# Four middle blocks of a retention-plus-MLP kernel: part of the first layer as seven products, and the next batch's retention all in the second layer

## The chip, the cores and the metric

One core of one Trainium2 chip. The metric is the device time of one execution of the whole kernel, in microseconds; three runs of the kernel before gave 293.72 us as the median (293.19 to 295.14). Inputs are float32, the matmuls work in float16 and accumulate in float32.

## The reference

Eight batches of eight heads, 576 positions, head width 64. Retention is attention without softmax, with a decay per head; its output, laid out as 4608 tokens of 512 values, goes through two weight matrices with a GELU between them:

```python
scores = (q @ k.T) / 8 ; ret = scores * Dmat        # Dmat[i, j] = gamma_h ** (i - j) for i >= j, else 0
x = (ret @ v).transpose(0, 2, 1, 3).reshape(4608, 512)
h = x @ w_in                                        # 512 x 2048
out = gelu_tanh(h) @ w_out                          # 2048 x 512
```

## The kernel before

The 4608 tokens are nine blocks of 512 (`NTB` = 9, counted t = 0 to 8). Block t below 8 holds the first 512 positions of batch t; block 8 holds the remaining 64 positions ("tails") of all eight batches. While TensorE runs the two layers of block t, the retention of batch t+1 is woven in between, so that `xT`, the retention's output, is there when block t+1 begins.

**First layer.** `up` (line 474) makes one of 16 column slices f of 128: four matmuls over 512 tokens into a bank `hp`, and a GELU on ScalarE into `gT`. Slices f and f + 8 belong together. Blocks 7 and 8 (`WIN`, line 514) make three of their four column groups (a group is two low and two high slices) in Strassen-Winograd form instead: `up_prod` (line 554) makes seven products of four matmuls over 256 tokens each, numbered 1 to 7, from sums of weight parts (`in_sums`, line 518) and of input parts (`x_sums`, line 535). Products share banks: 1, 6, 7, 4 accumulate one after the other in `hB`, 5 and 3 in `hC`, 2 is in `hA`. Between two of them the bank's intermediate value is read out: after 1 and 6 by a ScalarE copy, after 7 by a VectorE copy; VectorE then adds the other banks and ScalarE applies the GELU. `W_ORDER` (line 848) writes the order out by hand: "06" is product 6 of group 0, an empty token is one plain `up`, "a" and "b" are the sums below, "Q" a second-layer product.

**Second layer.** Always in seven products (`prod`, line 648), each two halves of eight matmuls over 256 columns; four sums per pair of slices prepare the left sides (`act_sums`, lines 642 to 646: s1, s2, a difference in place in `gT`, and s4). In blocks 1 to 6 the order is 1, 6, 5, 7, 2, 4, 3 (line 1036). Products 6, 7 and 4 accumulate in the one bank `opB`; after 6 VectorE adds it into k2 (line 721), after 7 into k3 and the output (lines 726 and 728), after 4 into the other output half.

**Retention of the next batch.** Four chunks of 128 positions, two at a time. `score` (line 379) takes two PSUM banks a chunk; `masks` (line 389) multiplies each by the decay mask on VectorE and so frees it; `past` and `av` (lines 436 and 455) make `xs` from the carried state `tbd` and the masked scores; `put` (line 466) copies `xs` to `xT` on ScalarE; `state`, `scan` and `spread` (lines 402, 416, 430; the last two together are `later`, line 784) carry the state from chunk to chunk, `spread` on ScalarE. There are eight PSUM banks, handed out in the order in which they were dropped (`bank`, line 61).

**What sets the order.** Every engine runs its instructions in the order of emission, and that order is written by hand. A block's steps are numbered u = 0 to 15 in the first layer and 16 to 29 in the second (one half product each); `at(t, u, f)` hangs work behind step u of block t. For blocks 2 to 6 line 949 puts the first two chunks' scores at u = 11 (blocks 2 and 3) or 9, their reads and the other two chunks' scores at 15, those masks at 17 and 19 and their reads at 24. So half of the masks, and the state of the first three chunks, fall into the first layer.

**Loads.** All float32 inputs arrive through one queue (SP) into a ring of 16 tiles of 128 x 512 (`LD`, tag "ld", line 71); `pump` (line 141) issues the next load as soon as a cast has freed a tile. The 12 tiles of batch b are cast during the second layer of block b - 2 from u = 16 on (`ut`, line 970): keys and queries on GpSimd, values on ScalarE. A tiny GpSimd copy, the `gate` (line 979), first waits for the last s4 sum. DMA transposes (`turn_dma`, line 305) follow. Tails of two batches come as further loads (`load_tails`), are cast on GpSimd behind the batches 4, 5 and 7 and in block 6 (`cast_tails`), and add their own scores, masks and reads in blocks 3, 4, 6 and 7 (`TP`, line 132).

Of the kernel before, what the change touches and what calls it, by code (L numbers as in the profile page):

```python
# [20 lines left out]
def kernel(  # L21
# [23 lines left out]
    LD = 16  # L45
# [3 lines left out]
    NT4 = 4  # L49
    scale = 1.0 / math.sqrt(D)  # L50
# [18 lines left out]

    def lds():  # L70
        return sb.tile([128, 512], F32, tag="ld", name="ld", bufs=LD)

# [66 lines left out]
    q_ld = {"next": 0, "free": LD, "hold": False}  # L139

    def pump(freed=0):
        q_ld["free"] += freed
        while q_ld["next"] < len(seq) and not q_ld["hold"]:
# [5 lines left out]
            if s[0] != "t":  # L149
                if q_ld["free"] == 0:  # L150
                    return
                q_ld["free"] -= 1
# [103 lines left out]
    def cast(b, key, c, eng):  # L256
        a = att[b]
        raw = a["raw"].pop((key, c))
# [255 lines left out]
    WIN = {t: 3 for t in (NTB - 2, NTB - 1)}  # L514
    GW = max(WIN.values())
    wi = {}

    def in_sums(j, ns):
        if not wi:
            for g in range(0, GW, 2):  # L520
                for n in "234":
                    wi[n, g // 2] = sb.tile([128, 2, 512], F16, tag="ld", name="wi" + n, bufs=LD)
# [12 lines left out]
    def x_sums(t):  # L535
        if not xw:
            for n in ("12", "34"):
                x = sb.tile([128, 2, 4, 2, TL], F16, tag="ld", name="x" + n, bufs=LD)
                xw[int(n[0])], xw[int(n[1])] = x[:, 0], x[:, 1]
            for n in range(3):  # L540
                for s in "svu" if n < 2 else "vu":
                    wk[s, n] = sb.tile([128, 512], F32, tag="ld", name="w" + s, bufs=LD)
# [3 lines left out]
        for s, x, y, f in (  # L546
# [3 lines left out]
            nc.vector.tensor_tensor(out=s, in0=x, in1=y, op=f)  # L550

    wk, wb, due = {}, {}, []

    def up_prod(t, j, m):
# [23 lines left out]
        s, v, u3 = wk["s", j % 2], wk["v", j % 3], wk["u", j % 3]  # L578
# [55 lines left out]
    def act_sums(t, f0, f1, us=slice(0, 2), parts=(0, 1)):  # L634
# [6 lines left out]
        if 0 in parts:  # L641
            nc.vector.tensor_tensor(out=s["1"], in0=a21, in1=a22, op=ALU.add)  # L642
            nc.vector.tensor_tensor(out=s["2"], in0=s["1"], in1=a11, op=ALU.subtract)
            nc.vector.tensor_tensor(out=a21, in0=a11, in1=a21, op=ALU.subtract)  # L644
        if 1 in parts:
            nc.vector.tensor_tensor(out=s["4"], in0=a12, in1=s["2"], op=ALU.subtract)  # L646
# [25 lines left out]
    def after(t, m, u):  # L672
# [46 lines left out]
        elif m == 6:  # L719
            keep["u2"] = sb.tile([128, 2, HD], F32, tag="k2", name="k2", bufs=1)  # L720
            add(keep["u2"], keep["s1"], pr("B"))
            for f in range(0, NH if t in WIN else 0, 2):
                act_sums(t, f, f + 2, parts=(1,))
        elif m == 7:
# [35 lines left out]
    def cast_w(kind, *i):  # L760
# [11 lines left out]
        pump(1)  # L772
# [4 lines left out]
    def cc(b, key, c, eng):  # L777
        cast(b, key, c, eng)
        pump(1)
# [70 lines left out]
    ).replace("p", "").split(" ")  # L850
    for n in range(GW):
        at(NTB - 3, 17 + 2 * n, lambda n=n: in_sums(n, (3, 2)))
        at(NTB - 3, 18 + 2 * n, lambda n=n: in_sums(n, (4, 1)))
    at(NTB - 3, 27, lambda: x_sums(NTB - 2))
# [60 lines left out]
    for t, b in TP.items():  # L915
        at(t, 3, lambda b=b: tail_values(b))
# [30 lines left out]
    for t in range(1, B):  # L947
        b, tl = t + 1, TP.get(t)
        s0, o0, s1, o1 = U2 if t == 1 else (11 if t in (2, 3) else 9, 15, 15, 24)
        at(t, s0, lambda t=t, tl=tl: scores(t, 0, tl))  # L950
# [5 lines left out]
        else:  # L956
            at(t, s1, lambda b=b: (score(b, 2), score(b, 3)))
            at(t, 17, lambda b=b: masks(b, 2))
            at(t, 19, lambda b=b: masks(b, 3))
# [7 lines left out]
    for b in range(NPE, B):  # L967
# [3 lines left out]
        if b == NPE + 1:  # L971
            ut = [16, 16, 17, 19, 19, 20, 22, 22, 23, 24, 24, 25]
        if b == NPE:
# [17 lines left out]
    for t in range(NTB):  # L991
# [9 lines left out]
        else:  # L1001
# [7 lines left out]
            todo = deque(f + h for f in range(2 * WIN.get(t, 0), NH) for h in (0, NH))  # L1009
            for w in (W_ORDER if t in WIN else ()):  # L1010
# [7 lines left out]
                def token(w):  # L1018
# [5 lines left out]
                    elif w[0] in "ab":  # L1024
                        act_sums(t, 2 * int(w[1]), 2 * int(w[1]) + 2, parts=("ab".index(w[0]),))
                    else:
                        up_prod(t, int(w[0]), int(w[1]))
                steps.append((mixed, 0 if w[:1] in ("a", "b", "Q") else 1 if w else 2))
# [56 lines left out]
```

## Time and profile before

| what | value |
|---|---|
| median of three runs | 293.72 us (293.19 to 295.14) |
| the profiled execution | 293.76 us |
| its span | 292.0 us |
| granted TensorE clock, mean | 0.996 |
| block 3, first plain group to the next block's | 114.70 to 145.31 us |
| block 4 | 145.31 to 175.76 us |
| block 5 | 175.76 to 205.53 us |
| block 6 | 205.53 to 236.16 us |
| block 7, three groups as products | 236.16 to 262.13 us |
| GpSimd busy | 100.0 us of the span (34%) |

The span runs from the first to the last instruction of the profiled execution; the device time is a little longer. The block limits are the starts of their first matmuls in the chain of waits. A timeline line reads: start, duration (or of several in a row, their total), engine, source line, operation, output <- inputs, shapes, count, and in square brackets how long the engine stood idle before it and who released it. PE is TensorE, DVE VectorE, ACT ScalarE, POOL GpSimd, SP the queue of the loads. Instructions of one engine overlap at their edges, so several in a row take less than the sum of their durations.

### The profile page before, as it was taken

To read this page: it belongs to the slowest core of one execution; us is meant where nothing else is said; L and a number is where in the kernel's file an instruction comes from. 1 tells how busy PE (TensorE), PEld (TensorE's weight loads), DVE (VectorE), ACT (ScalarE), POOL (GpSimd) and SP (SyncE) were. 2 spreads that over 40 slices of the span, in tenths; PEclk is the share of its full clock that TensorE was granted. 3 is DMA by queue.
4 is the path that set the end of the run, shared out by engine and by line. 5 is a ranking of instruction groups with operands and counts; after the bars stand their busy time and mean duration, and the time that the engine had idled before them with its cause. 6 is when DMAs were issued, how large, how long until landed. Compare 5 with 4: busy or idle time off the path is not lost.

```text
span 292.0 us, 7383 instructions
## 1 busy us (share of the span) xinstructions
PE 280.1 (96%) x3024; PEld 207.6 (71%) x3024; DVE 204.1 (70%) x409; ACT 169.8 (58%) x321; POOL 100.0 (34%) x128
## 2 busy tenths in 40 slices
PE   6889998999999999999999999999999999999993
PEld 2558877888874687468845884488548887887783
DVE  7796998666864874477548834784489968974863
ACT  5487754987249545964396647664666258507810
POOL 4589779910661175008500730068030000000000
PEclk9999999999999999999999999999999999999998
DMA  6999999989999999999999979997952030003013
GB/s 195 308 382 370 364 293 228 252 213 163 225 192 230 235 206 183 244 235 210 200 267 209 218 147 270 216 190 99 271 95 38 2 144 3 0 21 125 3 36 108
DMA packets 139585, 53.95 MB, mean 185 GB/s; under 512 B 118048, under 2 KB 131360, under 8 KB 139552
## 3 DMA queue, kind: packets, MB, share of 16 engines
q1 hardware_dynamic: 138960, 52.97, 80.4%
q8 instruction: 23, 0.38, 0.6%
q10 hardware_dynamic: 592, 0.52, 0.5%
q14 instruction: 10, 0.08, 0.1%
HBM read 36.70 MB, written 9.44 MB: 158 GB/s over the span
## 4 chain that ended last, share of the span: by engine, by line
PE 66%; SPq 8%; DMA 8%; ACT 5%; POOL 5%; DVE 5%; issue 1%; POOLq 0%; DVEq 0%; ACTq 0%
PE hp L480 18%; PE opB L665 11%; PE opA L665 8%; PE opC L665 7%; SPq L101 5%; DMA ld<-in_moe_w_in_dram 4%; PE hp L501 4%; PE hB L574 3%; SPq L96 3%; ACT gT L486 3%; PE xs L459 2%; POOL w_out_sb L771 2%; PE st L383 2%; DMA ld<-in_v_dram 2%; DMA ld<-in_q_dram 2%; PE hC L574 2%
## 5 line engine op out<-in xcount | busy, mean ns | idle before, releaser
L480 PE MATMUL hp<-xT,w_in_sb 128*128 128x512 f16 x352 | 79.1, 379 | 0.6 <-ACT xT L469 0.3
L486 ACT ACTIVATE gT<-hp 128x512 f16<-128x512 f32 x88 | 50.1, 600 | 22.6 <-PE hp L480 22.0
L480 PEld LDWEIGHTS <-w_in_sb 128*128 128x128 f16 x352 | 34.0, 98 | 39.0 <-issue 1.1
L665 PEld LDWEIGHTS <-gT 128*128 128x128 f16 x576 | 54.9, 98 | 8.9 <-issue 0.9
L665 PEld LDWEIGHTS <-s 128*128 128x128 f16 x432 | 42.2, 98 | 4.9
L642 DVE TENSOR_TENSOR s<-gT 128x512 f16<-128x512 f16 x36 | 15.6, 434 | 31.2 <-ACT gT L486 24.5
L665 PE MATMUL opA<-w_out_sb,gT 128*128 128x256 f16 x288 | 36.0, 273 | 0.6 <-ACT w_out_sb L771 0.4
L392 DVE TENSOR_TENSOR ret<-st,cm 128x512 f16<-128x512 f32 x48 | 30.2, 681 | 3.6 <-PE st L383 3.6
L469 ACT CAST xT<-xs 128x512 f16<-128x512 f32 x36 | 19.2, 590 | 20.4 <-PE xs L459 17.0
L501 PE MATMUL hp<-xT,w_in_sb 128*128 128x256 f16 x256 | 29.9, 273 | 0.9 <-POOL w_in_sb L771 0.5
L275 POOL TENSOR_TENSOR ck<-ld,sc 128x512 f16<-128x512 f32 x24 | 25.0, 1043 | 9.7 <-DMA ld<-in_k_dram 9.7
L501 PEld LDWEIGHTS <-w_in_sb 128*128 128x128 f16 x256 | 24.3, 98 | 5.2 <-POOL w_in_sb L771 2.3
L434 ACT CAST tbd<-ws 64x256 f16<-64x256 f32 x48 | 19.4, 403 | 14.8 <-DVE ws L425 14.2
L275 POOL TENSOR_TENSOR cq<-ld,sc 128x512 f16<-128x512 f32 x24 | 26.1, 1088 | 2.6 <-DMA ld<-in_q_dram 2.1
L665 PE MATMUL opB<-wt,gT 128*128 128x256 f16 x224 | 26.8, 273 | 0.0
L979 POOL COPY gate<-s 128x1 f16<-128x1 f16 x5 | 0.9, 190 | 74.6 <-DVE s L646 74.6
L262 ACT CAST cv<-ld 128x512 f16<-128x512 f32 x24 | 14.2, 618 | 17.2 <-DMA ld<-in_v_dram 17.1
L508 ACT ACTIVATE gT<-hp 128x512 f16<-128x512 f32 x32 | 18.3, 605 | 3.5 <-PE hp L501 3.3
L679 DVE TENSOR_TENSOR k<-k,opB 128x512 f32<-128x512 f32 x17 | 11.7, 686 | 11.7 <-PE opB L665 10.7
L644 DVE TENSOR_TENSOR gT<-gT 128x512 f16<-128x512 f16 x36 | 18.0, 499 | 0.0
L665 PE MATMUL opB<-wt,s 128*128 128x256 f16 x144 | 17.4, 273 | 0.0
L665 PE MATMUL opC<-wt,s 128*128 128x256 f16 x144 | 17.2, 272 | 0.0
(122 smaller groups left out, 406.4 us busy)
## 6 DMA issues: line engine op xcount, KB each, us to landing
ld<-in_q_dram SPq DMA_DIRECT2D x32, 256.0 KB, 5.2
ld<-in_k_dram SPq DMA_DIRECT2D x32, 256.0 KB, 5.1
ld<-in_v_dram SPq DMA_DIRECT2D x32, 256.0 KB, 5.3
out_dram<-ost SPq DMA_DIRECT2D x16, 512.0 KB, 3.9
ld<-in_moe_w_in_dram SPq DMA_DIRECT2D x16, 256.0 KB, 5.7
ld<-in_moe_w_out_dram SPq DMA_DIRECT2D x16, 256.0 KB, 5.6
lt<-in_k_dram SPq DMA_DIRECT2D x8, 128.0 KB, 4.7
lt<-in_q_dram SPq DMA_DIRECT2D x8, 128.0 KB, 4.4
```

Of the source, the lines that this page charges most:

```text
L101: nc.sync.dma_start(out=t.rearrange("p (h d) -> p h d", d=D), in_=src[b, :, 128 * c : 128 * c + 128, :].rearrange("h s d -> s h d"),)
L275: eng.tensor_tensor(out=dst.rearrange("p (h d) -> p h d", d=D), in0=raw.rearrange("p (h d) -> p h d", d=D), in1=sc[:, s0].unsqueeze(2).to_ ...
L392: nc.vector.tensor_tensor(out=r.rearrange("p (n i) -> p n i", i=128), in0=t.rearrange("p (n i) -> p n i", i=128), in1=(cm if b < PAIR else ...
L434: cp(out=(tbd[b % 2][r, c, :, r] if c < NC - 1 else tbt[b % NT4][r, :, r]), in_=w[r])
L469: nc.scalar.copy(out=xT[:, g0 : g0 + 2], in_=xs.rearrange("p (n g t) -> p g n t", n=HP, g=2))
L480: nc.tensor.matmul(hp.rearrange("p (g t) -> p g t", t=TL), w_in_sb[:, ct, 128 * fc : 128 * fc + 128], xT[:, o : o + TB // TL, ct, :], star ...
L486: nc.scalar.activation(out=gT[t][:, fc].rearrange("p i n -> p (i n)"), in_=hp, func=AF.Gelu_apprx_tanh)
L501: nc.tensor.matmul(hps[n][:, 256 * x : 256 * x + 256].rearrange("p (g t) -> p g t", t=TL), w_in_sb[:, ct, 128 * (fs[n] + x) : 128 * (fs[n] ...
L508: nc.scalar.activation(out=gT[t][:, f : f + 2, 2 * u : 2 * u + 2, :].rearrange("p f i n -> p f (i n)"), in_=hp.rearrange("p (f n) -> p f n ...
L642: nc.vector.tensor_tensor(out=s["1"], in0=a21, in1=a22, op=ALU.add)
L644: nc.vector.tensor_tensor(out=a21, in0=a11, in1=a21, op=ALU.subtract)
L665: nc.tensor.matmul(op[tag][:, HD * u : HD * u + HD], lhs(f), rhs[:, f], start=(new and f == 0), stop=(f == NH - 1), skip_group_check=True,)
```

## The change

Five things, all for blocks 3 to 6 (`MID`), with consequences in block 2 and in the rings.

1. **First layer.** Two of the four column groups become seven products each; the other eight slices stay plain. The order is `M_ORDER`: four plain slices, then products, then plain slices in between. A token such as "c21" is part of `act_sums` on VectorE: "c" is s1 and s2, "d" the difference in `gT`, the first digit is half of the first slice, the second half of the number of slices. After the last first-layer matmul come c01, c11, c31, d02, d31; s4 of all slices moves behind product 6 of the second layer.
2. **x sums** of these blocks run on GpSimd, hung at u = 0. Those of blocks 7 and 8 stay on VectorE.
3. **Retention** of the next batch moves into the second layer: scores of the first two chunks (and tails) at 15, their masks at 17, reads and the other scores at 22, those masks at 23 and 24, their reads at 26. The casts of the batch after next go from u = 16 to 20 and on.
4. **Weight sums** of the first two groups (`in_sums`) move from block 6 to block 2 (u = 17 to 20); the third stays in block 6. They stay on VectorE.
5. **Rings.** The ring of 16 becomes two of 8 ("ld", "lm"), taken in turn for the weights and batches 0 to 3; from batch 4 on only "ld" is used, and "lm" holds the weight sums, the x sums and work tiles of the products. The work tiles of group 0 share buffers with k1, k2 and k3.

Block 7's hand-written order gets one plain slice moved to its front. The core of the diff:

```diff
-    LD = 16
+    LD = 8
+    FIRST = 3
...
-                if q_ld["free"] == 0:
+                tag = "ld" if s[0] == "b" and s[1] >= FIRST + 1 else ("ld", "lm")[q_ld["n"] % 2]
+                if q_ld["free"][tag] == 0:
                     return
...
+    MID = {t: 2 for t in range(FIRST, NTB - 2)}
...
-            nc.vector.tensor_tensor(out=s, in0=x, in1=y, op=f)
+            (nc.gpsimd if t in MID else nc.vector).tensor_tensor(out=s, in0=x, in1=y, op=f)
...
+        def work(s):
+            n = j % (2 if s == "s" else 3)
+            if n == 0 and m == {"s": 1, "v": 6, "u": 7}[s]:
+                wk[s, 0] = sb.tile([128, 512], F32, tag=KT[s], name=KT[s], bufs=1)
+            return wk[s, n] if (s, n) in wk else None
...
             for f in range(0, NH if t in WIN else 0, 2):
                 act_sums(t, f, f + 2, parts=(1,))
+            for f in range(0, NH if t in MID else 0, 4):
+                act_sums(t, f, f + 4, parts=(1,))
...
+    M_ORDER = "    01 c21 02 05 11 06 12 d21  15 07 16  04 17 03  14 13  c01 c11 c31 d02 d31".split(" ")
     for n in range(GW):
-        at(NTB - 3, 17 + 2 * n, lambda n=n: in_sums(n, (3, 2)))
-        at(NTB - 3, 18 + 2 * n, lambda n=n: in_sums(n, (4, 1)))
-    at(NTB - 3, 27, lambda: x_sums(NTB - 2))
+        t, u = (FIRST - 1, 17 + 2 * n) if n < 2 else (NTB - 3, 15 + 2 * n)
+        at(t, u, lambda n=n: in_sums(n, (3, 2)))
+        at(t, u + 1, lambda n=n: in_sums(n, (4, 1)))
+    for t in MID:
+        at(t, 0, lambda t=t: x_sums(t))
+    at(NTB - 3, 29, lambda: x_sums(NTB - 2))
...
-        at(t, 3, lambda b=b: tail_values(b))
+        at(t, 16 if t in MID else 3, lambda b=b: tail_values(b))
...
-        s0, o0, s1, o1 = U2 if t == 1 else (11 if t in (2, 3) else 9, 15, 15, 24)
-        at(t, s0, lambda t=t, tl=tl: scores(t, 0, tl))
+        s0, o0, s1, o1 = U2 if t == 1 else (15, 22, 22, 26) if t in MID else (11 if t == 2 else 9, 15, 15, 24)
+        if t in MID:
+            late = [(b, 0), (b, 1)] + ([(PAIR + tl, 0)] if tl is not None else [])
+            at(t, s0, lambda late=late: [score(*w) for w in late])
+            at(t, 17, lambda late=late: [masks(*w) for w in late])
+        else:
+            at(t, s0, lambda t=t, tl=tl: scores(t, 0, tl))
...
-            at(t, 17, lambda b=b: masks(b, 2))
-            at(t, 19, lambda b=b: masks(b, 3))
+            at(t, s1 + (1 if t in MID else 2), lambda b=b: masks(b, 2))
+            at(t, s1 + (2 if t in MID else 4), lambda b=b: masks(b, 3))
...
+        if t0 in MID:
+            ut = [u + 4 for u in ut]
```

## The prediction

> **What bounds the kernel now.** I read the page's shares first, then the busy time of each engine block by block, then the chain of waits through block 4, then VectorE's and ScalarE's timelines of the same block, and last the places where GpSimd runs beside VectorE. A profiled execution took 293.76 us: a span of 292.0 us and 1.76 us around it. The median of the three runs is 293.72 us, so the sum below is made on 293.76 and serves for both.
>
> ```profile
> span 292.0 us, 7383 instructions
> ...
> PE 280.1 (96%) x3024; PEld 207.6 (71%) x3024; DVE 204.1 (70%) x409; ACT 169.8 (58%) x321; POOL 100.0 (34%) x128
> ```
>
> TensorE is busy for 96%. By blocks (block 4 and block 6 here; columns are the sum, then PE, PEld, DVE, ACT, POOL) it has no hole in the blocks that the change edits:
>
> ```profile
> 145.30:175.80 30.50, 30.50 (x310) 21.02 (x308) 18.92 (x38) 18.84 (x36) 8.96 (x10) 1.00 1.00 211
> ...
> 205.50:236.20 30.70, 30.43 (x295) 20.76 (x293) 25.04 (x54) 16.67 (x32) 2.48 (x2) 1.00 0.42 92
> ```
>
> So a shorter first layer pays only if the other engines still answer in time. The chain of waits through block 4 (start, us, what) gives the prices: a plain matmul over 512 columns goes at 8.63 / 40 = 0.216 us, a product matmul over 256 at 0.109 us.
>
> ```profile
> 145.31 8.63 PE hp L480 x40
> 153.95 0.78 PE st L383 x24
> 154.72 5.29 PE hp L480 x24
> ...
> 163.91 1.75 PE opB L665 x16
> 165.66 1.75 PE opC L665 x16
> 167.41 1.75 PE opB L665 x16
> ...
> 236.16 0.44 PE hB L574 x4
> ```
>
> The second opB entry is product 7. It accumulates onto the bank of product 6, so it may start only when VectorE has read product 6 out (the add into k2, line 721). VectorE's timeline shows that read today:
>
> ```profile
> 154.40 2.47 DVE L392 TENSOR_TENSOR ret<-st,cm 128x512 f16<-128x512 f32 x4
> 156.79 1.28 DVE L392 TENSOR_TENSOR ret<-st,tm 128x512 f16<-128x512 f32 x2
> ...
> 163.75 1.28 DVE L392 TENSOR_TENSOR ret<-st,cm 128x512 f16<-128x512 f32 x2
> 165.77 0.69 DVE L679 TENSOR_TENSOR k<-k,opB 128x512 f32<-128x512 f32 x1 [0.74 <-PE opB L665]
> ```
>
> The add waited for TensorE (0.74 us) and ended at 166.46, 0.95 us ahead of product 7. That 0.95 us is all the slack there is.
>
> **The work saved.** A plain column group is 16 x 0.216 = 3.45 us, as seven products 28 x 0.109 = 3.06 us. Eight groups change: 8 x 0.39 = **-3.1 us**. Four VectorE operations of 0.69 us and two ScalarE copies of 0.58 us come with each group. The four x sums of a block stand on GpSimd (nearest rows: its cast 0.61, its product 1.04 us; I take 1.04, it has two inputs). They end some 4 us into a block, where product 5 wants the first at 4.3 us: priced at nothing, covered by the four plain groups in front; each us past 4.3 would cost one.
>
> **Blocks 3 to 6, step by step.** ScalarE and VectorE at the start of block 4, and nine GELUs back to back (4.74 / 9 = 0.53 us apiece, 0.49 in the pair):
>
> ```profile
> 89.98 4.74 ACT L486 ACTIVATE gT<-hp 128x512 f16<-128x512 f32 x9
> ...
> 149.20 1.09 ACT L486 ACTIVATE gT<-hp 128x512 f16<-128x512 f32 x2
> ```
>
> ```profile
> 150.32 0.42 DVE L642 TENSOR_TENSOR s<-gT 128x512 f16<-128x512 f16 x1 [3.03 <-ACT gT L486]
> 150.78 0.42 DVE L643 TENSOR_TENSOR s<-s,gT 128x512 f16<-128x512 f16 x1
> 151.12 0.42 DVE L644 TENSOR_TENSOR gT<-gT 128x512 f16<-128x512 f16 x1
> ```
>
> I count r from the block's first matmul. Undisturbed, TensorE needs 8 x 0.865 + 14 x 0.437 = 13.0 us for the first layer, then 0.78 us of scores (0.55 without tails) and 1.75 us each for products 1, 6, 5; product 7 would start at r = 19.1.
>
> Step 1, ScalarE in the first layer. Block 4 ends its fourth GELU at 150.29 (r = 5.0), behind two pairs of state copies. The copy of product 1 then ends near 5.5, and product 6 of the same group may write its bank only after that; it is ready at 5.2. Next, VectorE has the sums of f 4 and 5 in front of the first product add, so the second copy ends near 8.1 while product 7 of the first layer is ready at 7.7. 0.35 + 0.4 = 0.75 us a block, **+3.0 us** in four (0 as in block 7, which runs the same product order without a gap of over 0.1 us but without state copies; 6 if VectorE is further behind).
>
> Step 2, the read-out of product 6. The last first-layer product ends at r = 12.9 and its add at 13.7. Its GELU stands on ScalarE behind five others whose first can start at 12.3; at 0.5 us apiece it ends at 15.5. Only then can VectorE go on, in its order: sums of f 2 and 3 (0.80: 150.32 to 151.12), of f 6 and 7 (0.80), the differences over eight tiles (0.85, from the 0.884 of a 128x1024 sum on line 630) and over four (0.35), the four masks (2.4, from 154.40 to 156.79), the two tail masks (1.2), and then the add into k2 (0.69). Behind that add stand the last s sums, and GpSimd's casts of the next batch wait for those. 15.5 + 7.1 = 22.6. TensorE is ready at 19.1 + 0.75 = 19.85. It waits 2.7 us in blocks 3, 4 and 6; in block 5, which has no tail masks, 1.7. Rounded down a little for the 128x1024 estimate: 2.6 x 3 + 1.7 = **+9.5 us** (6 to 11).
>
> Step 3, banks. Behind half of product 7 stand the reads (three xs banks, one us bank) and four score banks, with three banks still held by opA, opB and opC: the last score waits for ScalarE's copies of xs to xT (0.48 us apart, 1.56 for three): 0.4 us in three blocks, **+1.2 us** (0 to 2).
>
> Step 4, the state of the next chunk. It is now computed after the second score, not before the second layer. From the end of product 7: the k3 add and the output add behind it 0.09 + 0.72 + 0.61, two masks 1.2, vs 0.45, ws 0.42 (1.23 beside a cast on GpSimd), two copies to tbd 0.82, and 0.08 of handing over: 4.4 to 5.2 us. TensorE has product 2, half of product 4 and one read in that time: 1.75 + 0.87 + 0.22 = 2.85. It waits 1.5 to 2.3 us for the tbd of line 434; behind those copies ScalarE still has two value casts and the xT that the next block begins with, which then come just ahead of it (r = 34.6 to 35.2 in a block of some 35.4). GpSimd is still casting in blocks 3 to 5 (its gate waits for the s sums, r = 24.3, and eight casts follow), so 1.9 x 3 + 1.5 = **+7.2 us** (5 to 9).
>
> **Block 2.** Two thirds of the weight sums move here from block 6, where nothing waited for them, so nothing is won there. In block 2 GpSimd casts at the same time. What that does, tail casts beside sums in block 6:
>
> ```profile
> 213.60 0.42 DVE L643 TENSOR_TENSOR s<-s,gT 128x512 f16<-128x512 f16 x1
> 213.94 1.26 DVE L644 TENSOR_TENSOR gT<-gT 128x512 f16<-128x512 f16 x1
> 215.13 1.26 DVE L646 TENSOR_TENSOR s<-gT,s 128x512 f16<-128x512 f16 x1
> ```
>
> ```profile
> 213.64 2.48 POOL L275 TENSOR_TENSOR e<-lt,sc 128x512 f16<-128x512 f32 x2 [10.49 <-DMA lt<-in_k_dram]
> ```
>
> An f16 sum goes from 0.42 to 1.26 us beside a cast, one for one. Four such sums now stand ahead of the add into k2. Two beside casts and two free are 2 x 1.2 + 2 x 0.4 = 3.2 us, less the 0.74 us idle and 0.95 us slack: 1.5 us, and 0.8 us for the second four ahead of the k3 add: **+2.3 us** (0.5 if all run free, 4.5 if none does).
>
> **What I price at nothing.** Blocks 7 and 8 keep their products; one plain group moves to the front of block 7. No DMA is added, but loads 9 to 12 of batches 5 to 7 stand on SP behind GpSimd's first casts, and tail loads, one output and the transposes behind those. With the gate at r = 24.3 the last casts end near 33, the tail casts near 37, the transposes land some 8 us into the next block and the scores read them at 13.8: covered by some 6 us, past which each us costs one. The x sums would start near 37, with the block 35 us long: 2 us into the next block, first one done at 3, wanted at 4.3.
>
> Sum: -3.1 + 3.0 + 9.5 + 1.2 + 7.2 + 2.3 = +20.1 us, **313.9 us**.
>
> **Rivals.**
> Faster: VectorE reaches the add into k2 by r = 19.8. For it: its busy share is only 70% now, and block 7, with three product groups, shows no lasting gap. Against it: block 7 has no masks of the next batch there and reads products 4 and 2 ahead of 6. All waits have to stay below 3.1 / 4 = 0.78 us a block to decide; with none the time is 293.76 - 3.1 = 290.7. Chance 0.06; about no change 0.03.
>
> Mild: VectorE falls behind by less, because ScalarE's last GELU comes near 14 instead of 15.5 (its rows back to back are 0.49 us). Steps 2 and 4 halve: 20.1 - 8.35 = +11.75, or 305.5; with steps 1 and 3 at 0 and block 2 at 0.5 (6.0 less) 299.5. With shorter blocks the x sums come late instead (37 against a block of 32: the first at 6, wanted at 4.3, so 1.7 us in blocks 4 and 6), which keeps the low end from going lower. Chance 0.17.
>
> Worse: the TensorE clock. After the last matmul (line of the windows: stretch, sum, matmuls, granted clock) it averages 0.74; from the first filler on, with no hole over 0.8 us, it is 1.00.
>
> ```profile
> 288.00:292.00 4.00, 0.00 (x0) 0.74 0.59 179
> ```
>
> A wait of 2.7 us may let it fall. If the 128x256 matmuls then cost 0.218 us for as long as the wait itself, each of the three waits adds 1.35 us: +4; for the remaining 10 us of each block, +15: 318 to 329. The Trainium skill (TensorE: Matmul & The Clock Gate, section What's actually happening) says that the clock is halved after one idle window of about 3.4 us and needs as long a busy one to return. By that rule the waits here stay just under the window, and the trace, which has no such hole, cannot show it. Chance 0.10.
>
> The forecast itself, 305.5 to 322: chance 0.64. A measurement of this kernel can tell about 1% from no change. The range of **302 to 323** takes in the forecast, half of the mild case and the near end of the clock case, some 0.78 together. Slower by over 1%: 0.91; within 1%: 0.03; faster: 0.06.
>
> **What would show it.** Step 2: in blocks 3 to 6 opB (product 7) idle before it, put down to the DVE k add, some 2 us each; the six masks in one row directly ahead of that add. Step 4: the xs read of the last chunk (line 450 now) waits for ACT tbd, 1.5 to 2.3 us. Step 1: hB waits for the ACT copies, under 0.5 us each. Block 2: wi sums of 1.2 us and a later second opB. Blocks of some 35 us (33 for block 5) instead of 30.5. I am wrong if opB follows opC without a hole, if masks run before the last sums, or if TensorE waits mainly for GpSimd's x sums or for loads.

## The result, and the profile after

| what | before | after |
|---|---|---|
| median of four runs | 293.50 us | 320.43 us (317.60 to 321.30) |
| ratio after to before, 95% interval | | 1.0888 (1.0806 to 1.0971) |
| the profiled execution | 293.76 us | 319.68 us |
| block 2 | 30.27 us | 31.69 us |
| blocks 3, 4, 5, 6 | 30.45, 30.45, 29.77, 30.63 | 37.22, 38.35, 34.27, 35.61 |
| block 7 | 25.97 us | 26.75 us |

The kernel is slower by 26.9 us. The direction and the range were right, the predicted 313.9 us are 6.5 us short. Ratios leave out disturbed executions; among the runs below this touches one execution of one kernel. Block limits here and below are the starts of each block's first matmul in the timeline. Line numbers below are those of each kernel's own program; of the changed kernel, masks are line 404, the adds of the second layer 700, the activation sums 667, the state copies 446, the ScalarE copies of products 1 and 6 of the first layer 615 and 621.

The page of the changed kernel, its span and first row:

```profile
span 317.8 us, 7666 instructions
...
PE 283.8 (89%) x3120; PEld 217.2 (68%) x3120; DVE 224.3 (71%) x429; ACT 175.3 (55%) x337; POOL 119.2 (38%) x144
```

TensorE is busy for hardly longer than before (280.1 us), and the span is 25.8 us longer: nearly all of it is standing still. The list of TensorE's waits (who waited, for whom: total us, times, longest) says where:

```profile
PE opB L686 <- DVE k L700: 7.7, 5, 1.8
PE xs L462 <- ACT tbd L446: 7.6, 5, 1.9
PE hB L589 <- ACT k L621: 3.1, 5, 1.4
...
PE hB L589 <- ACT k L615: 2.0, 4, 1.0
PE st L395 <- ACT xT L481: 1.1, 4, 0.3
```

The first row is step 2 (four times) and block 2 (once), the second step 4, the third and fourth step 1, the last a part of step 3. None of the first, third and fourth was there before; the second stood at 0.8 us in one place. By blocks 3 to 5 (window, its length, then PE, PEld, DVE, ACT, POOL busy, granted clock, DMA share, GB/s):

```profile
115.55:152.77 37.22, 31.17 (x335) 23.20 (x333) 24.77 (x43) 19.23 (x38) 16.16 (x17) 1.00 0.86 171
152.77:191.12 38.35, 32.71 (x335) 24.28 (x333) 24.82 (x44) 20.08 (x41) 16.19 (x17) 0.96 0.71 146
191.12:225.39 34.27, 30.53 (x310) 22.40 (x308) 22.17 (x41) 19.10 (x39) 11.87 (x13) 1.00 0.87 176
```

TensorE now has 4 to 6 us of holes in each, where it had none; no other engine comes near being full. The holes come from the order on VectorE. Its timeline in block 3, around the end of the first layer:

```profile
132.55 0.42 DVE L667 TENSOR_TENSOR s<-gT 128x512 f16<-128x512 f16 x1 [0.61 <-ACT gT L606]
...
134.15 1.02 DVE L667 TENSOR_TENSOR gT<-gT 128x1024 f16<-128x1024 f16 x2
135.08 2.47 DVE L404 TENSOR_TENSOR ret<-st,cm 128x512 f16<-128x512 f32 x4
137.48 1.28 DVE L404 TENSOR_TENSOR ret<-st,tm 128x512 f16<-128x512 f32 x2
138.67 0.67 DVE L700 TENSOR_TENSOR k<-k,opB 128x512 f32<-128x512 f32 x1
139.27 1.28 DVE L667 TENSOR_TENSOR s<-gT,s 128x1024 f16<-128x1024 f16 x2
144.28 0.69 DVE L700 TENSOR_TENSOR k<-k,opB 128x512 f32<-128x512 f32 x1 [3.73 <-PE opB L686]
```

The late sums, six masks, the add into k2 and the last s sums: one row of work without a gap, as predicted, 8.0 us long (132.55 to 140.55), and straight behind it 3.73 us in which VectorE has nothing to do. TensorE in the same block, product 7 and the last chunk's read of the past:

```profile
139.40 1.03 PE L686 MATMUL opB<-wt,gT 128*128 128x256 f16 x8 [1.68 <-DVE k L700]
...
148.99 0.40 PE L462 MATMUL xs<-tt,tbd 128*128 128x128 f16 x4 [1.90 <-ACT tbd L446]
```

And the clock in block 4, in windows of 1 us (the last three columns: granted clock, DMA share, GB/s):

```profile
185.00:186.00 1.00, 0.24 (x4) 0.23 (x4) 1.00 (x2) 0.96 (x3) 0.75 (x1) 1.00 0.00 0
186.00:187.00 1.00, 1.00 (x23) 0.91 (x22) 0.05 (x1) 1.00 (x3) 0.00 (x0) 0.59 0.00 0
187.00:188.00 1.00, 1.00 (x21) 0.81 (x18) 0.00 (x0) 1.00 (x3) 0.00 (x0) 0.50 0.07 16
...
190.00:191.00 1.00, 1.00 (x11) 0.90 (x10) 0.97 (x3) 0.00 (x0) 1.00 (x2) 1.00 0.00 0
```

Behind the 1.84 us hole that ends at 185.76 the clock is halved for 3.4 us.

**A table of stages.** Times between starts of TensorE's work in block 3, in us. "Undisturbed" is what the same matmuls need with no wait: 8 plain slices at 0.865 and 14 products at 0.437 for the first layer, the rest from the block before the change. The stages left out are the same in all columns, but for 0.3 us at product 1 with four edits.

| stage | undisturbed | after | early state | late masks | both | four edits | retention only |
|---|---|---|---|---|---|---|---|
| first layer (step 1) | 13.04 | 15.25 | 14.15 | 14.15 | 14.28 | 13.94 | 13.91 (plain) |
| product 6 to product 7 (step 2) | 3.50 | 6.06 | 6.06 | 4.23 | 4.23 | 4.26 | 3.99 |
| half of 7, reads | 2.46 | 2.46 | 2.46 | 3.61 | 3.61 | 3.61 | 2.46 |
| scores, to the other half (step 3) | 0.55 | 1.34 | 1.34 | 0.96 | 0.96 | 0.96 | 1.34 |
| last reads (step 4) | 1.36 | 3.44 | 1.51 | 3.11 | 1.36 | 1.36 | 3.03 |

The columns on the right are experiments, told next.

### The profile page after: what moved, and what is told of

It is laid out like the page before. It is cut to its first block, busy times and chain, and to the rows that moved or that the text cites. A ratio compares the mean times of both kernels' runs of the same rounds, so it can differ in the third digit from the quotient of the medians.

```text
span 317.8 us, 7666 instructions
## 1 busy us (share of the span) xinstructions
PE 283.8 (89%) x3120; PEld 217.2 (68%) x3120; DVE 224.3 (71%) x429; ACT 175.3 (55%) x337; POOL 119.2 (38%) x144
## 5 line engine op out<-in xcount | busy, mean ns | idle before, releaser
L492 PE MATMUL hp<-xT,w_in_sb 128*128 128x512 f16 x224 | 53.3, 379 | 0.0
L667 DVE TENSOR_TENSOR s<-gT 128x512 f16<-128x512 f16 x36 | 16.7, 463 | 27.2 <-ACT gT L498 15.9
L686 PE MATMUL opB<-wt,gT 128*128 128x256 f16 x224 | 29.0, 278 | 7.7 <-DVE k L700 7.7
L686 PE MATMUL opA<-w_out_sb,gT 128*128 128x256 f16 x288 | 35.3, 273 | 0.5 <-ACT w_out_sb L794 0.4
L492 PEld LDWEIGHTS <-w_in_sb 128*128 128x128 f16 x224 | 21.8, 98 | 20.1
L498 ACT ACTIVATE gT<-hp 128x512 f16<-128x512 f32 x56 | 32.0, 597 | 3.5 <-PE hp L492 3.1
L287 POOL TENSOR_TENSOR ck<-ld,sc 128x512 f16<-128x512 f32 x24 | 25.8, 1076 | 8.9 <-DMA ld<-in_k_dram 8.9
L513 PEld LDWEIGHTS <-w_in_sb 128*128 128x128 f16 x256 | 24.3, 98 | 5.3 <-POOL w_in_sb L794 2.3
L589 PEld LDWEIGHTS <-w_in_sb 128*128 128x128 f16 x224 | 21.9, 98 | 5.5 <-issue 0.3
L589 PEld LDWEIGHTS <-wi 128*128 128x128 f16 x168 | 15.7, 98 | 11.7 <-ACT k L621 3.6
L589 PE MATMUL hB<-x,wi 128*128 128x256 f16 x112 | 15.9, 273 | 5.1 <-ACT k L621 3.1
L520 ACT ACTIVATE gT<-hp 128x512 f16<-128x512 f32 x32 | 18.4, 604 | 3.5 <-PE hp L513 3.3
```

The costliest lines, as they stand in the source:

```text
L287: eng.tensor_tensor(out=dst.rearrange("p (h d) -> p h d", d=D), in0=raw.rearrange("p (h d) -> p h d", d=D), in1=sc[:, s0].unsqueeze(2).to_ ...
L492: nc.tensor.matmul(hp.rearrange("p (g t) -> p g t", t=TL), w_in_sb[:, ct, 128 * fc : 128 * fc + 128], xT[:, o : o + TB // TL, ct, :], star ...
L498: nc.scalar.activation(out=gT[t][:, fc].rearrange("p i n -> p (i n)"), in_=hp, func=AF.Gelu_apprx_tanh)
L513: nc.tensor.matmul(hps[n][:, 256 * x : 256 * x + 256].rearrange("p (g t) -> p g t", t=TL), w_in_sb[:, ct, 128 * (fs[n] + x) : 128 * (fs[n] ...
L520: nc.scalar.activation(out=gT[t][:, f : f + 2, 2 * u : 2 * u + 2, :].rearrange("p f i n -> p f (i n)"), in_=hp.rearrange("p (f n) -> p f n ...
L589: nc.tensor.matmul(pb[:, 256 * i : 256 * i + 256].rearrange("p (g t) -> p g t", t=TL), w(kt, i), x(kt), start=(new and i == kt == 0), stop ...
```

## The experiments

My theory: the order on VectorE, and ScalarE behind it, holds TensorE at the four places of the table, each place by its own queue. The rivals: one of these waits only hides another; the products themselves, GpSimd's part, or the loads are to blame; the clock makes the difference. The products of the first layer alone, with the retention in its old place, were not run, so what they would gain or cost by themselves is not shown.

**Early state.** In blocks 3 to 6:

```diff
-        at(t, o0 + 1, lambda b=b: later(b, 2))
+        at(t, o0 + (0 if t in MID else 1), lambda b=b: later(b, 2))
-            at(t, s1 + (1 if t in MID else 2), lambda b=b: masks(b, 2))
+            at(t, s1 + (0 if t in MID else 2), lambda b=b: masks(b, 2))
```

> In blocks 3 to 6 VectorE takes the state of the third chunk (scan) and that chunk's two masks directly behind the scores, in the 3.7 us in which it now waits for product 7, and no longer behind the k3 add. Theory (VectorE's order sets the wait of step 4): the 7.6 us that TensorE waits at the xs read for ACT tbd fall below 1.5 us, the granted clock stays at 1.00 in block 4 because its 1.84 us hole is gone, and the time is 320.4 - 7.5 - 1.7 = 311.2 us (310 to 314). Rival (the wait only moves): the k3 add now comes behind the two masks, product 4 waits for it before it may write opB, and at most 3 us come back: 317 us or more.

Measured: 315.34 us, ratio 1.0749 (1.0715 to 1.0783), below the changed kernel's interval. The profile's waits:

```profile
PE opB L686 <- DVE k L700: 8.5, 5, 2.6
PE hB L589 <- ACT k L621: 4.5, 5, 1.8
...
PE xs L462 <- ACT tbd L446: 0.8, 1, 0.8
```

The 7.6 us for tbd are down to the 0.8 us that the kernel before had too. Summed over the four blocks, the stage of the last reads goes from 13.26 to 5.43 us, which is undisturbed (5.44). The wait did not move to the k3 add: the rival falls. The total is 4 us above what I expected: in this profile block 2 has a hole of 2.6 us and half clock behind it (34.03 us long), and the first layer is 0.5 to 1.4 us longer in blocks 4 to 6.

**Late masks.**

```diff
-            at(t, 17, lambda late=late: [masks(*w) for w in late])
+            at(t, 17, lambda late=late: masks(*late[0]))
+            at(t, 19, lambda late=late: [masks(*w) for w in late[1:]])
```

> In blocks 3 to 6 only the first chunk's two masks stay ahead of the k2 add; the other two and the two tail masks run behind it. Theory (step 2 is VectorE's queue ahead of that add, 0.6 us a mask): four masks fewer ahead of the add in blocks 3, 4 and 6 and two fewer in block 5 take 2.4 and 1.2 us off, so the 7.7 us put down to opB waiting for DVE k fall below 2 us; 0.5 us a block comes back as a wait of the reads for masks and banks: 320.4 - 8.4 + 2 = 314 us (312 to 317). Rival (the sums of the last group set it, not the masks): opB still waits 1 us or more in each block, 318 us or more.

Measured: 318.68 us, ratio 1.0848 (1.0812 to 1.0884), not to be told from the changed kernel by time alone. The waits:

```profile
PE xs L462 <- ACT tbd L446: 7.3, 5, 1.9
PE opB L686 <- DVE k L700: 3.3, 1, 3.3
...
PE xs L462 <- DVE ret L404: 1.5, 3, 1.1
...
PE xs L471 <- DVE ret L404: 0.9, 4, 0.4
PE opC L686 <- DVE ret L404: 0.8, 3, 0.3
```

In blocks 3 to 6 product 7 waits no more for the k2 add; the one opB wait left is block 2's. So the masks ahead of that add do make the wait, but taking them away gives back only a part: the reads now wait for masks. By the table, step 2 falls by 1.83 us in block 3 and the reads grow by 1.15, the scores fall by 0.38: 1.1 us a block. Of the 2.56 us that step 2 had cost there, 0.73 stay (2.7 us over the four blocks): product 6 starts in time but runs haltingly while the last s sums are made, and product 5 waits for a bank that a mask must free (the last row). In the changed kernel the later k2 add covers this. In block 5, without tail masks, nothing is left of it (34.41 against 34.27 us). Both theory and rival had half of it.

**Both.**

> The early state and the late masks together. Each alone made blocks 3 to 6 shorter in its profile, 145.45 us in sum after the change: 137.9 with the early state, 140.3 with the late masks. Theory (the two waits lie behind each other and are independent, only the clock's 1.75 us in block 4 is counted in both): 145.45 - 7.5 - 5.2 + 1.75 = 134.5 us for the four blocks and 309.5 us in all (307.5 to 311.5). Rival (VectorE has no room: the masks now late run into the place of the early state): 313 us or more.

Measured: 309.64 us, ratio 1.0571 (1.0517 to 1.0625); blocks 3 to 6 take 133.53 us (134.5 expected), and the time lies inside the range. The two edits add up, so steps 2 and 4 are queues of their own.

**The first layer: three edits of one suspect each.** GpSimd's x sums back on VectorE; the c21 sums behind product 2 of the second group; the copies of the state, with their scans, away from the block's start:

```diff
-            (nc.gpsimd if t in MID else nc.vector).tensor_tensor(out=s, in0=x, in1=y, op=f)
+            nc.vector.tensor_tensor(out=s, in0=x, in1=y, op=f)
```
```diff
-    M_ORDER = "    01 c21 02 05 11 06 12 d21  15 ...
+    M_ORDER = "    01 02 05 11 06 12 c21 d21  15 ...
```
```diff
-                at(t + 1, c, lambda c=c, nb=b + 1: later(nb, c))
+                at(t + 1, c + (8 if t + 1 in MID else 0), lambda c=c, nb=b + 1: later(nb, c))
```

> The x sums of blocks 3 to 6 go back to VectorE, four of some 0.42 us at the start of each block. Theory (step 1 is dear in block 3 because the c21 sums stand beside GpSimd's x sums at 0.69 and 1.26 us; in the other blocks ScalarE is late): about 1 us comes back in block 3 and nothing elsewhere, 319.4 us (318.5 to 320.5). Rival one (GpSimd's sums are what makes step 1 dear everywhere): 3 us or more come back, 317.5 us or less. Rival two (VectorE is the engine that is short): 1.7 us more on VectorE in each block make it slower, 322 us or more.

> In blocks 3 to 6 the two s sums over f 4 and 5 (c21), which stand on VectorE ahead of the first product add, go behind product 2 of the second group. Theory (half of step 1 is VectorE coming late to that add, which makes the second ScalarE copy late): the 3.1 us that product 7 of the first group waits for that copy fall below 1.5 us, the 2.0 us for the first copy stay, 320.4 - 1.8 = 318.6 us (317.5 to 319.5). Rival (ScalarE's own queue makes the second copy late): both waits stay, 320 us or more.

> The states of chunks 0 and 1 of the next batch (two scans on VectorE, four copies on ScalarE), which stand at the start of blocks 3 to 6, go eight steps later, into the middle of the product groups; the x sums stay on GpSimd. Theory (step 1's first half is ScalarE, late with the copy of product 1 because of these four copies): the 2.0 us of product 6 waiting for that copy go to below 0.5, and the second wait shrinks too, 320.4 - 2.5 = 318 us (317 to 319.5). Rival (in the middle they hold up other adds and GELUs as much): 320 us or more.

Measured: 322.83 us (ratio 1.1012, 1.0942 to 1.1081), 320.23 us (1.0948, 1.0904 to 1.0992) and 319.38 us (1.0924, 1.0860 to 1.0988). None is told from the changed kernel by time, whose spread is larger than what each moves; the third median lies in its forecast range, the first two do not, and both lie where a rival put them. The waits tell more. In block 3 of the changed kernel the c21 sums, beside GpSimd's x sums, keep the first product add back:

```profile
120.69 0.69 DVE L667 TENSOR_TENSOR s<-gT 128x512 f16<-128x512 f16 x1 [2.93 <-ACT gT L498]
121.42 1.26 DVE L667 TENSOR_TENSOR s<-s,gT 128x512 f16<-128x512 f16 x1
122.60 0.67 DVE L602 TENSOR_TENSOR k<-k,hA 128x512 f32<-128x512 f32 x1
```

In blocks 4 to 6 the x sums are over or nearly over by then, and the c21 sums take 0.42 to 0.54 us. With the x sums on VectorE (first fence) the wait for the second copy shrinks, but the first grows from 2.0 to 5.0 us: the x sums now stand ahead of the states on VectorE, and ScalarE gets to its state copies, and behind them to the copy of product 1, about 1 us later (block 3). With c21 late (second fence) the second copy's wait falls from 3.1 to 0.6 us:

```profile
PE hB L589 <- ACT k L615: 5.0, 4, 1.3
...
PE hB L589 <- ACT k L621: 1.9, 5, 0.5
```

```profile
PE hB L589 <- ACT k L615: 2.1, 4, 0.8
...
PE hB L589 <- ACT k L621: 0.6, 1, 0.6
```

With the state copies late the first copy's wait is gone from the list, and 1.9 us for the second plus 1.4 us for that of the other group remain. The four first layers together take 58.8 us after the change, 60.2, 57.3 and 56.4 us in these three, against 52.2 undisturbed. So both causes that the prediction named have a part in step 1, ScalarE's state copies and VectorE's sums; GpSimd's part is a trade, not a gain. They are not all of it: with both edits in (the four edits below) the first layers still take 55.5 us, so half of the 6.6 us is left, and the scores that follow take 1.15 us more.

**Retention alone.** Plain first layer, weight sums back in block 6:

```diff
-            todo = deque(f + h for f in range(2 * {**WIN, **MID}.get(t, 0), NH) for h in (0, NH))
+            todo = deque(f + h for f in range(2 * WIN.get(t, 0), NH) for h in (0, NH))
...
-            for f in range(0 if t == 1 or t in WIN or t in MID else NH):
+            for f in range(0 if t == 1 or t in WIN else NH):
```

> Blocks 3 to 6 have eight plain groups in the first layer again, as before the change, and the weight sums stand in block 6 again; the retention of the next batch stays in the second layer. Theory (step 2 needs the late sums and the masks together, steps 3 and 4 need only the moved retention): opB waits for the k2 add no more, the wait for tbd stays near 7.5 us and that for xT near 3, steps 1 and the saving are gone: 293.5 + 7.5 + 3 = 304 us, with the clock's share 306 (302 to 308). Rival one (the products carry the cost): 298 us or less. Rival two (the masks alone hold up the k2 add): 311 us or more.

Measured: 307.72 us, ratio 1.0495 (1.0457 to 1.0532). The moved retention alone costs 14.2 us, more than half of everything:

```profile
PE xs L462 <- ACT tbd L446: 6.7, 5, 1.5
PE opB L686 <- DVE k L700: 3.0, 3, 2.3
```

Step 4 stays nearly whole, step 3 too (the table), and step 2 falls to 0.5 us in blocks 3 and 4 and to nothing in block 5, since the sums are done by then: it needs the late sums and the masks together. The 2.3 us are block 6 alone, where three groups of weight sums now meet the masks; I had not foreseen that.

**The rest alone.**

```diff
-    MID = {t: 2 for t in range(FIRST, NTB - 2)}
+    MID = {}
...
-(11 if t == 2 else 9, 15, 15, 24)
+(11 if t in (2, 3) else 9, 15, 15, 24)
```

`MID` is empty, so that only the rings, block 2's weight sums and block 7's order stay of the change. The plain groups of blocks 3 to 6 then read weights that block 2's sums have replaced in place: shape and count of all operations are those of the kernel before, the values are not.

> Blocks 3 to 6 as before the change (plain first layer, retention in its old places); what stays of the change is the two load rings of eight, two thirds of the weight sums in block 2, and the order of block 7. Theory (of these only block 2, 1.4 to 2.3 us, and block 7, up to 0.8 us, cost anything; loads and rings nothing): 293.2 + 2.2 = 295.5 us (294 to 297.5), with block 2 at 31.7 us or, if three or four sums fall beside a cast, up to 34.9. Rival (rings of eight make loads late and the casts with them): waits for ld in front of the transposes or the scores, 299 us or more.

Measured: 297.57 us (295.50 to 299.92), ratio 1.0136 (1.0050 to 1.0223). Blocks 3 to 6 take 30.45, 30.45, 29.77 and 30.20 us: the same as before the change to 0.01 us in three of them, so rings and loads cost nothing in this run. The time is 0.07 us above the forecast range. All of it is block 2, 34.09 us, and block 7, 26.69. In block 2:

```profile
102.48 1.26 DVE L543 TENSOR_TENSOR wi<-w_in_sb 128x512 f16<-128x512 f16 x1
103.77 1.15 DVE L543 TENSOR_TENSOR wi<-wi,w_in_sb 128x512 f16<-128x512 f16 x1
...
106.04 0.41 DVE L543 TENSOR_TENSOR wi<-w_in_sb,wi 128x512 f16<-128x512 f16 x1
106.37 1.26 DVE L543 TENSOR_TENSOR w_in_sb<-w_in_sb 128x512 f16<-128x512 f16 x1
107.56 0.67 DVE L700 TENSOR_TENSOR k<-k,opB 128x512 f32<-128x512 f32 x1
```

```profile
108.28 3.46 PE L686 MATMUL opB<-wt,gT 128*128 128x256 f16 x16 [2.61 <-DVE k L700]
```

Three of the four sums stand beside a cast here and take 1.15 to 1.26 us; the third ran in the gap in which GpSimd waited for a load. In the changed kernel's profile two did (a wait of 1.76 us), with the late masks and with the four edits below all four (3.3 us). So the moment at which a load lands decides how many, and block 2 is 31.7 to 36.0 us long in profiles of kernels that have the same instructions there. Executions of one kernel differ by up to 4.7 us (317.86 to 322.51 with the state copies late), and by 7.8 with the weight sums later (below); that this is block 2 in each of them is likely and not shown. And product 7 itself takes 3.46 us here in place of 1.91: half clock.

**The weight sums later in block 2**, behind its k3 add:

```diff
-        t, u = (FIRST - 1, 17 + 2 * n) if n < 2 else (NTB - 3, 15 + 2 * n)
+        t, u = (FIRST - 1, 23 + 2 * n) if n < 2 else (NTB - 3, 15 + 2 * n)
```

> The eight weight sums of block 2 go behind the k3 add of that block (steps 23 to 26 in place of 17 to 20). Theory (product 7 of block 2 waits because four of them stand ahead of the k2 add, each 0.42 us alone and up to 1.26 us beside a GpSimd cast; 1.8, 2.6 and 3.3 us of wait in the three profiles so far as two, three or four stood beside a cast, the longer two with the clock at half speed behind them): that wait goes, block 2 is back at 30.3 us instead of 31.7 to 34.9, 320.4 - 2 = 318.4 us, 1.4 to 4 us back (316.4 to 319). Rival (the sums are in the way there too, ahead of the output adds and the states of batch 4): less than 1 us back, 319.5 us or more.

Measured: 319.67 us (319.05 without the longest execution), ratio 1.0888 (1.0831 to 1.0945): no gain. The profile is of that longest execution, 324.60 us at a clock of 0.982. Block 2 is 29.77 us long in it, its wait is gone as the theory has it; but the sums now end at 119.1, ahead of the last two output adds and the states, and in block 3 TensorE waits 3.2 us for the copy of product 1:

```profile
124.57 1.03 PE L589 MATMUL hB<-x,wi 128*128 128x256 f16 x4 [3.17 <-ACT k L615]
```

There the rival holds: paid in the next block. That the three shorter executions pay at the same place is likely, since their ratio is the changed kernel's, and not shown.

**Work for the idle TensorE.** Six matmuls of 128x512 that nobody reads, in front of product 7 and of the last read:

```diff
+    def fill(n):
+        t = bank("fill")
+        for _ in range(n):
+            nc.tensor.matmul(t, ident, w_out_sb[:, 0], start=True, stop=True)
+        drop(t)
...
+fill(6) if (m, u) == (7, 0) and 2 <= t < NTB - 2 else None
...
+            if c == 2 and t in MID and w[1] == 3:
+                fill(6)
```

> The changed kernel with six idle-time matmuls of 128x512 (1.3 us, into a bank that nobody reads) put on TensorE ahead of product 7 in blocks 2 to 6 and ahead of the last chunk's read of the past in blocks 3 to 6, where it stands still for 1.6 to 3.3 us anyway. Nothing else changes. Theory (the runs of one kernel spread, and block 4 or block 2 of a profile is 1.7 us or more longer, because a hole of TensorE may be followed by 3 to 4 us at half clock): with at most 0.6 us of each hole left (1.3 to 2 in the worst block 2) the granted clock is 0.997 or more in nearly all executions and the time 317.5 us (316.5 to 318.5). Rival (the clock falls for another reason): clocks of 0.98 to 0.99 remain and the time stays at 319.5 to 321.

Measured: 320.58 us (clocks 0.997, 1.000, 0.999, 0.991), ratio 1.0935 (1.0857 to 1.1013). Its profile shows no drop of the clock between 80 and 300 us and no hole over 2 us, but one execution still has a clock of 0.991, and the time is what it was, also in the three at 0.997 or more: the rival's range, not the theory's. So the clock is not what makes the changed kernel slow; what it takes, 1.6 us in the changed kernel's profile, is too little against this spread to be seen in medians.

**Four edits together** (state, masks, c21, copies), and then block 2's sums on GpSimd in the first half of that block:

```diff
-            nc.vector.tensor_tensor(out=o, in0=x, in1=y, op=f)
+            (nc.gpsimd if j < 2 else nc.vector).tensor_tensor(out=o, in0=x, in1=y, op=f)
...
-        at(t, u, lambda n=n: in_sums(n, (3, 2)))
-        at(t, u + 1, lambda n=n: in_sums(n, (4, 1)))
+        at(t, 4 + 2 * n if n < 2 else u, lambda n=n: in_sums(n, (3, 2)))
+        at(t, 10 + 2 * n if n < 2 else u + 1, lambda n=n: in_sums(n, (4, 1)))
```

> Four of the edits together: early state, late masks, the c21 sums late, the state copies of the block start late. The first two together gave 309.6 us; the trace then shows 3.1 and 2.2 us of the first layer's waits for the two ScalarE copies, 3 us of reads waiting for masks, and block 2. Theory (step 1 is the sum of those two waits): up to 4 us of them come back, 306 us (304.5 to 308). Rival (VectorE has by then no room left, and what is put off holds up the k2 add or the masks): 308.5 us or more. In either case it stays above the kernel before, 293 us, since block 2 and the reads' wait for masks remain.

> The four edits of the run before, and the eight weight sums of block 2 on GpSimd, in the first half of that block, where GpSimd stands still for 11 us ahead of its casts (at some 1.15 to 1.33 us a sum, 10 us in all). Theory (block 2's cost, 31.7 to 36.0 us instead of 30.3 with half clock behind the longer holes, comes only from these sums standing on VectorE ahead of the k2 add beside casts): block 2 is at 30.3 to 30.8 us, the clock stays at 1.00 there, and the 307.6 us of the four edits become 304 us (302.5 to 305.5). Rival (on GpSimd they slow VectorE's activation sums of block 2 and so the same add, or push the casts back): block 2 at 31.5 us or more, 306.5 us or more.

Measured: 307.56 us (ratio 1.0487, 1.0414 to 1.0559) and 307.20 us (1.0443, 1.0404 to 1.0482). Blocks 3 to 6 take 132.09 and 132.15 us, 13.4 and 13.3 less than after the change, but only 1.4 less than with the first two edits alone: of the up to 4 us that the theory wanted back from the first layer, about a third came. The second time misses its forecast, and its rival holds. In the second, block 2 has 31.49 us and no wait for the k2 add, against 35.96 with a 3.25 us hole and 6.8 us of half clock in the first one's profile. But VectorE's own sums in block 2 now stand beside GpSimd's:

```profile
93.41 1.26 DVE L667 TENSOR_TENSOR s<-s,gT 128x512 f16<-128x512 f16 x1
94.59 1.37 DVE L667 TENSOR_TENSOR gT<-gT 128x512 f16<-128x512 f16 x1
95.88 1.37 DVE L667 TENSOR_TENSOR s<-gT,s 128x512 f16<-128x512 f16 x1
```

The masks behind them are late, and the reads wait 1.06 us for them. The medians don't tell the two kernels apart; the four executions of the second lie closer together (306.46 to 308.14 us, clocks of 0.996 and more, against 306.30 to 310.46). No version with the moved retention came near the kernel before.

## Why the prediction was right, and where it was short

The working against the profile of the changed kernel, in us, summed over blocks 3 to 6 by the stages of the table where it concerns them:

| step | predicted | measured |
|---|---|---|
| work saved | -3.1 | -3.5 (plain first layer 13.91 in the retention-only run, products 13.04) |
| step 1, first layer | +3.0 (0 to 6) | +6.6 (58.8 - 52.2) |
| step 2, k2 add | +9.5 (6 to 11) | +9.3 |
| step 3, banks of the scores | +1.2 (0 to 2) | +3.05 |
| step 4, state of the next chunk | +7.2 (5 to 9) | +7.3 |
| block 2 | +2.3 (0.5 to 4.5) | +1.4; with the clock behind it +3.8 in another profile |
| clock in block 4 | a rival, +4 to +15 | +1.6 |
| block 7 | 0 | +0.8 |

The sum is 26.5 us against 25.9 between the two profiled executions; block 2 starts 0.57 us earlier than before.

**Right.** Steps 2 and 4, two thirds of the sum, in place, cause and size. The add into k2 ends 6.8 us behind the last GELU of the first layer (132.52 to 139.34), for which the prediction had counted 7.1 instruction by instruction. The state's queue, from the k3 add to the read of tbd, takes 4.7 us (144.28 to 148.99), predicted 4.4 to 5.2 from the end of product 7, which lies just ahead of it. Moving what was named takes all of step 4 away and 6.6 of the 9.3 us of step 2; the other 2.7 us come back under another name, at product 5.

That step 2 hits its size so well is partly luck. The prediction lets step 1 delay TensorE by 0.75 us but not the last GELU, which stands behind the same layer; carried through, its own working gives 3.5 us a block in place of 2.7, 13 us in all. Against that, the last GELU ended 1.7 us behind the first layer (130.80 to 132.52) and not 2.5 (15.5 - 13.0). The two slips cancel.

**Too small: step 1.** The two hold-ups are those of the prediction, and their sizes hold but for one block each. Product 6 waits 0.28, 1.03, 0.37 and 0.35 us in blocks 3 to 6 (predicted 0.35), product 7 1.41, 0.31, 0.32 and 0.43 (predicted 0.4). The 1.41 us of block 3 are the c21 sums beside GpSimd's x sums (1.26 in place of 0.42 us), which I priced at nothing although I had shown that price for block 2. The 1.03 us of block 4 come with a later row on ScalarE: the copy of product 1 starts 5.75 us into the block, in the others at 5.0 to 5.1. Together these are 4.5 of the 6.6 us (the 5.1 of the list less block 7's 0.6). I let the layer run undisturbed from there; it does not: the rest lies in gaps too short for the list, in part because the list counts a wait from the modelled end of the matmul before, some 0.17 us late (product 7 in block 3: 1.41 us listed, but 2.02 from the start of four matmuls that need 0.44). What makes them was not tried.

**Too small: step 3.** 0.4 us a block came from ScalarE's three xT copies alone. Measured 0.57 to 0.85: the trace shows 0.11 and 0.28 us in block 3 at two scores that wait for xT (142.40 and 142.89), the rest is shorter. The late masks lower it to 0.25 to 0.47, probably because the reads ahead of it are then the later ones. How it divides further was not tried.

**Too large: block 2.** The four weight sums ahead of the k2 add cost what was counted, a wait of 1.76 us where the working had 1.5; the 0.8 us for the other four, ahead of the k3 add, did not come.

**Not priced: block 7.** TensorE waits 0.6 us there for the copy of product 6 of group 0, at 265.69. The plain slice that stood between products 2 and 5 of group 1, ahead of that wait, is the one that the new order moved to the front of the block; this is read from the order and was not tried alone.

**The rivals.** *Mild* supposed steps 2 and 4 at half; they came whole. *Faster* needed waits below 0.78 us a block; the four edits together still leave 3.6 (132.09 us against 121.30 - 3.5, over four). *Worse* was right that the clock may fall and wrong in size: 1.6 us here, and in block 2 of other profiles 1.5 to 2.8, an estimate: those blocks are 34.03 to 35.96 us long with holes of 2.60 to 3.26 us, against 31.69 with a hole of 1.76 us and the full clock. I had kept it apart because each wait stays under the window of 3.4 us that the Trainium skill gives (TensorE: Matmul & The Clock Gate, section What's actually happening). The traces differ: see below.

## What to carry to other kernels

A cheaper matmul schedule is worth what the engines that read its results can follow: count, for each bank that is accumulated in parts, what stands in the queue of the engine that must read it in between, and put nothing ahead of that read that could stand behind it. Where an engine has a row without a gap and a long wait directly behind it (8.0 us, then 3.73), the order is wrong before the load is: moving the state into that wait gave the whole 7.3 us of step 4 back. But moving work behind a read helps only if nobody waits for it there: of the 1.83 us that block 3 won at product 7 by late masks, 0.8 came back as waits elsewhere.

## What the hardware showed

**The clock falls behind holes that are shorter than its window.** Over the profiles of the changed kernel and its variants, between 80 and 300 us, TensorE stood still for 1.2 to 2.0 us at 60 places, and twice the clock fell with it (holes of 1.84 and 1.89 us); a hole of 2.34 us had no effect; the six of 2.6 to 3.3 us all brought a granted clock of 0.50. It stayed there for 3.41 us, twice for 6.83. So the Trainium skill's "idle window (~3.4µs)" (TensorE: Matmul & The Clock Gate, section What's actually happening) is not needed in full.

Which hole does it depends on where it lies, more than on its length. In the traces' records of the clock, all eight falls between 80 and 290 us come at a whole multiple of 3.413 us behind the rise before: 30 of them four times, 31, 34 and 53, and 7 for the second fall in one profile. Counted in windows laid like this, TensorE stood still for 1.84 to 3.25 us in the eight windows that end in a fall and for at most 1.79 us in all others but one. That one has 1.96 us, and its hole ends 0.02 us ahead of the window's end; why it had no effect is open. The holes of 1.83 and 1.84 us at the place of block 4's, with the state copies or the c21 sums late, had no fall behind them: a border cuts them, 1.62 and 1.77 us lie in one window. The hole of 2.34 us is cut too, and the two windows hold 1.35 and 1.33. No run moved a hole on purpose to test this.

**VectorE and GpSimd take turns, wherever the sums are put.** A 128x512 float16 sum with two inputs takes 0.42 us on VectorE alone and 1.15 to 1.37 us where a GpSimd instruction runs beside it throughout, less where only in part; GpSimd's own takes 1.15 to 1.33. That agrees with the exclusive lock in the Trainium skill (SBUF — State Buffer, section Who interferes with whom). Masks, with one input in PSUM, keep their 0.6 us (two in 1.27 us beside GpSimd's casts in block 2). Moving such sums between the two engines moves the price; it does not pay it.
